# Value products of two attention heads side by side: one PSUM accumulation a pair, softmax denominators on VectorE

## Chip, cores, metric

One core of one Trainium2 chip runs the whole program. The metric is device time in microseconds (us), the median of the runs. The kernel before takes 1075.93 us (three runs, 1074.74 to 1076.09).

## What is computed

Eight batches of eight heads, 512 local and 32 global tokens, head size 64. Every global token attends to all 544 keys; a local token attends to the 32 global keys and to local keys at most 32 positions away. The attention output (4352 rows of 512) then goes through a two-layer network with a softplus between.

```python
s_g = scale * np.matmul(q_g, k_all.transpose(0, 1, 3, 2))
out_g = np.matmul(sm(s_g), v_all)
mask = np.abs(pos[:, None] - pos[None, :]) <= window        # window = 32
s_ll = np.where(mask, scale * (q_l @ k_l^T), -1e9)
a_l = sm(np.concatenate([s_lg, s_ll], axis=-1))
out_l = np.matmul(a_l, np.concatenate([v_g, v_l], axis=2))
...
h = x @ w_in
g = np.maximum(h, 0.0) + np.log1p(np.exp(-np.abs(h)))
return g @ w_out
```

`sm` is a softmax that subtracts the row's maximum and divides by the sum of the exponentials plus 1e-9.

## The kernel before

**Network.** TensorE does the two layers in three products each of single-pass fp32r (L533 to L535 and L556 to L558): high and low halves of each operand, the low by low product left out. Per batch there are 16 steps `f`: `hpart` (12 matmuls of 512 columns into `h`), `act` (L537: Abs, Exp, Ln on ScalarE, one VectorE instruction that reads `h` again, a rounded copy `gh` on ScalarE, and the remainder `gl` on GpSimd), and `opart` (12 matmuls of 512 columns into `o`), two steps behind. In the first batch of the network the weights are still being turned from float64 bit patterns into fp32 halves (L474 to L498, four VectorE instructions a chunk).

**Attention.** Heads are taken two at a time; pair m is heads 2m and 2m+1 of the list of 64, four pairs a batch. Pairs 0 to 3 have code of their own ahead of everything, which the change leaves alone. Pairs 4 to 31 are interleaved with the network. Each is cut into three query windows p = 0, 1, 2 (288, 288 and 192 columns, 32 of them the global queries), and each window has two key chunks of 128 keys. All scores are transposed: keys on partitions, queries on columns.

- `scores(m, p)` (L286): the heads lie on the two row halves (partitions 0 to 63 and 64 to 127) of the operands, four matmuls a window in plain fp32. The result `s_ps` is one PSUM tile of two banks. From pair 8 on VectorE adds the mask while it copies to `s` in SBUF (L315), and a transposing reduction takes the maxima of blocks of 32 keys into `mt` (L316).
- `maxima(m)` (L326): once all three windows are there, GpSimd moves the block maxima to 32 partitions (L329) and VectorE combines them per query (L332 to L339). `probs(m, p)` (L343): a transposing copy spreads them over the partitions (`mb`, L347), GpSimd subtracts (L352 to L355), ScalarE takes the exponential in place (L356).
- `values(m, p)` (L358): two key chunks for each of two heads, four matmuls a window. The stationary operand is the value chunk with a column of ones, 128 by 65, so that row 64 of the result `v_ps` is the denominator. The two heads go to different banks. ScalarE copies the first window to `x` and the rest of the others (L369, L373), and VectorE adds the 64 overlapping queries and the 32 global ones (L374, L375).
- `combine(m)`, `invert(m)`, `normalise(m)`: the denominators go by DMA to `rec_scratch` in DRAM and back as 38 by 32 (`sc`), are inverted (L391, L392), written back, and read once more, broadcast to 64 partitions (`rb`, L396). VectorE multiplies, one instruction a head (L404), into `xa`. The global queries' columns go to `xg_scratch`.

`s_ps` and `v_ps` share one two-bank buffer, tag `a` of `ps_a`, with one copy: each user waits for the previous one to be read.

**Order.** Pieces of attention are written into the stream of network items by due times: `scores(m, p)` at 12m+4p, with maxima and probs behind the third window; `values(m, p)` at 12m+4p+22 (`LAG`); invert 3 and normalise 6 (`STEP`) behind the last. A batch of the network spans 48 units, and `first` (L632) sets the unit at which the second batch starts, so that the four pairs of a batch are normalised by the time `split_x` (L439) makes that batch's operands `xh` and `xl`. Pieces due before 69 (`START`) go ahead of the network. Within an engine the program runs in order; a scheduler places the instructions by its own estimates.

Of the kernel before, what the change touches and what calls it, by code (L numbers as in the profile page):

```python
# [53 lines left out]
def moe_over_global_local_attention(  # L54
# [225 lines left out]
    def load_v(m):  # L280
        t = pl.tile([P, 2, 6, 66], F32, tag="v", name=f"v{m}", bufs=2)
        nc.gpsimd.memset(t[:, :, :, D:D + 1], 1.0)
        nc.sync.dma_start(out=t[:, :, :, 0:D], in_=v[m - M0].rearrange("p (h c d) -> p h c d", h=2, d=D))
        st["v", m] = t

    def scores(m, p):  # L286
# [17 lines left out]
        if p == 0:  # L304
            st["mt", m] = pl.tile([P, 348], F32, tag="mt", name=f"mt{m}", bufs=2)
            nc.gpsimd.memset(windows(st["mt", m], 0, 36, 3, 3), LOW)
# [19 lines left out]
    def maxima(m):  # L326
        mt = st.pop(("mt", m))
# [3 lines left out]
        for u, du, off in ((0, 1, -2), (3, 1, 3)):  # L331
            nc.vector.tensor_reduce(grid(mt, e0 + u, (7, 6), (du, 2)), grid(mt, 3 + u, (12, 6), (du, 2), (off, 2), (GW, 4)), axis=AX.XY, op=ALU.max)  # L332
# [25 lines left out]
    def values(m, p):  # L358
        s, vt = st.pop(("s", m, p)), st["v", m]
        ps = ps_a.tile([P, 2, 512], F32, tag="a", name=f"v_ps{m}_{p}")  # L360
        parts = ((0, 0, 192), (192, 96, 192 if p < 2 else 96))
        for h in range(2):
            for i, (o, qs, w) in enumerate(parts):
                mm(ps[:65, h, qs:qs + w], lhsT=vt[:, h, 2 * p + i, 0:65], rhs=s[:, h, o:o + w],
                   start=i == 0, stop=i == 1, skip_group_check=True)

        if p == 0:
            st["x", m] = pl.tile([65, 2, 608], F32, tag="x", name=f"x{m}", bufs=2)
            nc.scalar.copy(st["x", m][:, :, 0:288], ps[0:65, :, 0:288])  # L369
# [3 lines left out]
        nc.scalar.copy(x[:, :, o + 64:o + w], ps[0:65, :, 64:w])  # L373
        nc.vector.tensor_tensor(x[:, :, o:o + 64], x[:, :, o:o + 64], ps[0:65, :, 0:64], op=ALU.add)  # L374
# [4 lines left out]
    SEG = ((lambda t: t[:, 32:160].unsqueeze(1), 0, 1, 128), (lambda t: windows(t, 192, 224, 2, 192), 128, 2, 192))

    def combine(m):
        nc.sync.dma_start(out=rec_dram[2 * m:2 * m + 2], in_=st["x", m][64:65])

        rows = rec_dram[2 * m:2 * m + 2].rearrange("h (s k) -> (h s) k", k=32)
        sc = pl.tile([38, 32], F32, tag="sc", name=f"sc{m}", bufs=1)
        nc.sync.dma_start(out=sc, in_=rows)
        st["sc", m] = sc, rows

    def invert(m):
        sc, rows = st.pop(("sc", m))  # L390
        after(nc.vector.tensor_scalar(sc, sc, 1e-9, None, op0=ALU.add), "scores")  # L391
        nc.vector.reciprocal(sc, sc)  # L392
        nc.sync.dma_start(out=rows, in_=sc)
# [352 lines left out]
```

## Time and profile before

| | |
|---|---|
| median of the runs | 1075.93 us |
| profiled execution, first to last instruction (span) | 1072.0 us |
| TensorE busy | 1014.0 us, 95% |
| VectorE busy | 596.9 us, 56% |
| ScalarE busy | 546.3 us, 51% |
| GpSimd busy | 460.8 us, 43% |
| mean granted TensorE clock | 0.982 |

The page gives only the span of the profiled execution, no total of its own. The median is 3.9 us above it; that difference is what lies around the span, and it is taken to stay. In the profile PE is TensorE, PEld its weight loads, DVE VectorE, ACT ScalarE, POOL GpSimd, SP the queue of DMA issues. Each plain fp32 matmul shows as two instructions (672 of `v_ps` in the trace for 336 in the program), each fp32r matmul as one. The length of a matmul row includes the way through the array; how much of TensorE's time one takes is read from the distance between starts.

### The profile page before, as it was taken

To read this page: it belongs to the slowest core of one execution; us is meant where nothing else is said; L and a number is where in the kernel's file an instruction comes from. 1 tells how busy PE (TensorE), PEld (TensorE's weight loads), DVE (VectorE), ACT (ScalarE), POOL (GpSimd) and SP (SyncE) were. 2 spreads that over 40 slices of the span, in tenths; PEclk is the share of its full clock that TensorE was granted. 3 is DMA by queue.
4 is the path that set the end of the run, shared out by engine and by line. 5 is a ranking of instruction groups with operands and counts; after the bars stand their busy time and mean duration, and the time that the engine had idled before them with its cause. 6 is when DMAs were issued, how large, how long until landed. Compare 5 with 4: busy or idle time off the path is not lost.

```text
span 1072.0 us, 14176 instructions
## 1 busy us (share of the span) xinstructions
PE 1014.0 (95%) x5108; PEld 801.9 (75%) x5108; DVE 596.9 (56%) x1138; ACT 546.3 (51%) x968; POOL 460.8 (43%) x526
## 2 busy tenths in 40 slices
PE   6895788899999999999999999999999999999996
PEld 4674566677777777777777777777777778888895
DVE  5978698976555655565555654565556542311211
ACT  6856555455445544545444544454444544554452
POOL 2226476653345444445444334544445541322321
PEclk9998899999999999999999999999999999999999
DMA  9523233313221312222221321231222210200000
GB/s 361 169 78 100 97 128 98 96 47 97 51 53 51 95 43 57 49 76 77 57 58 47 97 55 48 55 90 44 57 54 70 67 29 13 72 1 1 10 32 20
DMA packets 78565, 75.05 MB, mean 70 GB/s; under 512 B 53380, under 2 KB 57476, under 8 KB 78496
## 3 DMA queue, kind: packets, MB, share of 16 engines
q1 hardware_dynamic: 77952, 74.09, 23.5%
q8 instruction: 40, 0.66, 0.3%
q14 instruction: 29, 0.24, 0.1%
q10 hardware_dynamic: 544, 0.07, 0.0%
HBM read 64.43 MB, written 9.71 MB: 69 GB/s over the span
## 4 chain that ended last, share of the span: by engine, by line
PE 72%; DVE 10%; DMA 4%; issue 3%; POOL 1%; ACT 1%; SPq 0%; DVEq 0%; POOLq 0%; ACTq 0%
PE h L126 30%; PE o L126 29%; PE v_ps L126 8%; PE s_ps L126 5%; DMA rb<-rec_scratch 3%; DVE xa L404 2%; DVE xl L452 1%; DVE s L315 1%; DMA rec_scratch<-sc 1%; DVE wbitswo L489 1%; DVE xh L451 1%; DVE woraw L492 1%; DVE mb L347 0%; DVE e L543 0%; DVE wbitswo L486 0%
## 5 line engine op out<-in xcount | busy, mean ns | idle before, releaser
L126 PE MATMUL h<-xh,wi 128*128 128x512 f32 (+1 forms) x1152 | 356.4, 393 | 15.7 <-DVE xl L228 9.2
L126 PE MATMUL o<-wo,gh 128*128 128x512 f32 x1088 | 345.1, 398 | 0.0
L547 POOL TENSOR_TENSOR gl<-e,gh 128x512 fp32r<-128x512 f32 x136 | 177.3, 1304 | 386.4 <-ACT gh L546 318.2
L126 PEld LDWEIGHTS h<-xh,wi 128*128 128x128 f32 x1152 | 209.0, 190 | 62.8 <-issue 14.7
L126 PEld LDWEIGHTS o<-wo,gh 128*128 128x128 f32 x1088 | 199.9, 188 | 44.8 <-issue 5.2
L126 PE MATMUL h<-xl,wi 128*128 128x512 f32 (+1 forms) x576 | 220.3, 382 | 2.8 <-DVE xl L452 2.8
L126 PE MATMUL o<-wo,gl 128*128 128x512 f32 x544 | 213.4, 392 | 0.0
L540 ACT ACTIVATE e<-h 128x512 f32<-128x512 f32 x136 | 81.3, 598 | 240.1 <-PE h L126 238.6
L543 DVE SCALAR_TENSOR_TENSOR e<-h,e 128x512 f32<-128x512 f32 x136 | 93.2, 685 | 172.7 <-ACT e L542 167.7
L352 POOL TENSOR_TENSOR s<-s,mb 128x384 f32<-128x384 f32 x112 | 139.0, 1272 | 14.0 <-DVE mb L347 14.0
L546 ACT CAST gh<-e 128x512 fp32r<-128x512 f32 x136 | 83.9, 617 | 97.6 <-DVE e L543 97.5
L126 PEld LDWEIGHTS h<-xl,wi 128*128 128x128 f32 x576 | 109.4, 190 | 27.3 <-DVE xl L452 5.4
L126 PEld LDWEIGHTS o<-wo,gl 128*128 128x128 f32 x544 | 102.2, 188 | 22.8
L126 PE MATMUL v_ps<-s,v 128*65 128x192 f32 (+1 forms) x672 | 114.2, 313 | 4.2 <-DVE s L315 3.9
L126 PEld LDWEIGHTS v_ps<-s,v 128*65 128x65 f32 x672 | 88.5, 137 | 28.0 <-DVE s L315 5.9
L315 DVE TENSOR_TENSOR s<-s_ps,mask 128x768 f32<-128x768 f32 (+1 forms) x96 | 65.0, 696 | 76.6 <-PE s_ps L126 76.6
L356 ACT ACTIVATE s<-s 128x768 f32<-128x768 f32 (+1 forms) x84 | 66.5, 792 | 68.9 <-POOL s L352 45.6
L542 ACT ACTIVATE e<-e,one 128x512 f32<-128x512 f32 x136 | 98.3, 723 | 3.1
L126 PE MATMUL s_ps<-raw 64*128 64x192 f32 (+1 forms) x672 | 78.6, 347 | 14.0 <-issue 9.0
L541 ACT ACTIVATE e<-e 128x512 f32<-128x512 f32 x136 | 85.7, 630 | 3.6
L126 PEld LDWEIGHTS s_ps<-raw 64*128 64x128 f32 x672 | 53.3, 188 | 44.9 <-issue 33.4
L316 DVE TRANSPOSE_TENSOR_REDUCE mt<-s 128x24 f32<-128x768 f32 (+1 forms) x84 | 76.1, 907 | 10.7 <-ACT s L311 8.7
(144 smaller groups left out, 831.7 us busy)
## 6 DMA issues: line engine op xcount, KB each, us to landing
raw<-in_qk SPq DMA_DIRECT2D x56, 272.0 KB
v<-in_v SPq DMA_DIRECT2D x28, 384.0 KB
out<-ot SPq DMA_DIRECT2D x34, 256.0 KB
rb<-rec_scratch SPq DMA_DIRECT2D x28, 304.0 KB
wiraw<-in_w_in SPq DMA_DIRECT2D x16, 512.0 KB
woraw<-in_w_out SPq DMA_DIRECT2D x16, 512.0 KB
raw<-in_qk SPq DMA_DIRECT2D x28, 224.0 KB
v<-in_v SPq DMA_DIRECT2D x4, 512.0 KB
```

Source lines behind the costliest of these rows:

```text
L126: order["pe"] = after(nc.tensor.matmul(*a, **k), "pe").ins
L315: nc.vector.tensor_tensor(s[:, :, o:o + w], ps[:, :, o:o + w], mk.unsqueeze(1).to_broadcast([P, 2, w]), op=ALU.add)
L316: order["scores"] = nc.vector.tensor_reduce(windows(mt, 3 + 12 * p, 36, 2, nb), s.rearrange("p h (b k) -> p h b k", k=32), axis=AX.X, op=A ...
L352: nc.gpsimd.tensor_tensor(sw, sw, windows(mb[:, h], 0, 96, 2, 192), op=ALU.subtract)
L356: nc.scalar.activation(s, s, AF.Exp, scale=0.125)
L404: after(nc.vector.tensor_tensor(y[64 * h:64 * h + 64], x[0:64, h], rb[:, h], op=ALU.mult), "scores")
L540: nc.scalar.activation(e, ph, AF.Abs)
L541: nc.scalar.activation(e, e, AF.Exp, scale=-1.0)
L542: nc.scalar.activation(e, e, AF.Ln, bias=one)
L543: nc.vector.scalar_tensor_tensor(e, ph, 0.0, e, op0=ALU.max, op1=ALU.add)
L546: nc.scalar.copy(gh, e)
L547: nc.gpsimd.tensor_tensor(gl, e, gh.bitcast(F32), op=ALU.subtract)
```

## The change

The value products of a pair become one piece. For each of seven parts (a key chunk with the query columns it serves) there is one matmul a head, with 64 stationary columns and no column of ones. Head 0 writes PSUM partitions 0 to 63, head 1 partitions 64 to 127, at the same columns of the same bank, so that the two use the two column halves of the array. The 608 result columns of a pair lie side by side in two banks (384 and 224): overlapping queries of neighbouring windows add up in PSUM, and only the three copies of the global queries stay apart. The ScalarE copies and the VectorE additions go.

The denominators come from the exponentials in SBUF. `sums(m)` runs a transposing VectorE reduction for each window (the maxima's instruction with add for max), gathers and combines as `maxima` does, adds 1e-9, takes four reciprocals of 32 by 21, and spreads them with one transposing copy to `rb`, 128 by 608, no longer through DRAM. VectorE then multiplies straight out of PSUM, one instruction a bank, into `xa`; GpSimd adds the three copies of the global columns. `rec_scratch`, its four DMAs a pair, and the memset of the ones are gone.

Due times: `sums(m)` at 12m+14, `values(m)` with the multiplication at 12m+21. `first` falls from 72 to 60, so the first batch of the network holds the pieces due from 69 to 108 instead of 69 to 120.

```diff
-LAG = 22
+LAG_Z = 6
+LAG_V = 13
...
     def load_v(m):
-        t = pl.tile([P, 2, 6, 66], F32, tag="v", name=f"v{m}", bufs=2)
-        nc.gpsimd.memset(t[:, :, :, D:D + 1], 1.0)
-        nc.sync.dma_start(out=t[:, :, :, 0:D], in_=v[m - M0].rearrange("p (h c d) -> p h c d", h=2, d=D))
+        t = pl.tile([P, 2, 6, D], F32, tag="v", name=f"v{m}", bufs=2)
+        nc.sync.dma_start(out=t, in_=v[m - M0].rearrange("p (h c d) -> p h c d", h=2, d=D))
...
-    def maxima(m):
-        mt = st.pop(("mt", m))
+    def gather(mt, op):
         for a in range(1, 4):
             nc.gpsimd.tensor_copy(mt[0:32, GW * a:GW * a + GW], mt[32 * a:32 * a + 32, 0:GW])
...
+        return mt[:, e0:e0 + 44]
+
+    def maxima(m):
+        e = gather(st.pop(("mt", m)), ALU.max)
...
-    def values(m, p):
-        s, vt = st.pop(("s", m, p)), st["v", m]
-        ps = ps_a.tile([P, 2, 512], F32, tag="a", name=f"v_ps{m}_{p}")
-        parts = ((0, 0, 192), (192, 96, 192 if p < 2 else 96))
-        for h in range(2):
-            for i, (o, qs, w) in enumerate(parts):
-                mm(ps[:65, h, qs:qs + w], lhsT=vt[:, h, 2 * p + i, 0:65], rhs=s[:, h, o:o + w],
-                   start=i == 0, stop=i == 1, skip_group_check=True)
...
+    def sums(m):
+        zt = pl.tile([P, 348], F32, tag="mt", name=f"zt{m}", bufs=3)
+        nc.gpsimd.memset(windows(zt, 0, 36, 3, 3), 0.0)
+        for p in range(NPC):
+            nb = 12 if p < 2 else 9
+            nc.vector.tensor_reduce(windows(zt, 3 + 12 * p, 36, 2, nb), st["s", m, p].rearrange("p h (b k) -> p h b k", k=32),
+                                    axis=AX.X, op=ALU.add, apply_transpose=True)
+        z = gather(zt, ALU.add)
+        nc.vector.tensor_scalar(z[0:32, 0:42], z[0:32, 0:42], 1e-9, None, op0=ALU.add)
+        zr = pl.tile([P, 21], F32, tag="zr", name=f"zr{m}", bufs=2)
+        for a in range(4):
+            h = a // 2
+            nc.vector.reciprocal(zr[32 * a:32 * a + 32], z[0:32, 21 * h:21 * h + 21])
+        rb = st["rb", m] = pl.tile([P, 608], F32, tag="rb", name=f"rb{m}", bufs=1)
+        nc.vector.transpose(rb.rearrange("p (s k) -> p s k", k=32), zr[:, 1:20].unsqueeze(2).to_broadcast([P, 19, 32]))
+
+    def values(m):
...
+        ps = ps_a.tile([P, 2, 512], F32, tag="a", name=f"v_ps{m}")
+        parts = ((0, 0, 32, 160, 0, 0), (1, 0, 192, 192, 0, 64), (2, 1, 0, 192, 0, 192), (3, 1, 192, 96, 0, 288),
+                 (3, 1, 288, 96, 1, 0), (4, 2, 0, 192, 1, 32), (5, 2, 192, 96, 1, 128))
+        seen = set()
+        for c, p, o, w, bank, at in parts:
+            for h in range(2):
+                mm(ps[64 * h:64 * h + 64, bank, at:at + w], lhsT=vt[:, h, c], rhs=st["s", m, p][:, h, o:o + w],
+                   start=(bank, h) not in seen, stop=(c, bank) in ((3, 0), (5, 1)), skip_group_check=True)
+                seen.add((bank, h))
...
+        for bank, at, w in ((0, 0, 384), (1, 384, 224)):
+            nc.vector.tensor_tensor(y[:, at:at + w], ps[:, bank, 0:w], rb[:, at:at + w], op=ALU.mult)
+        for o in (352, 576):
+            nc.gpsimd.tensor_tensor(y[:, 128:160], y[:, 128:160], y[:, o:o + SG], op=ALU.add)
+        nc.sync.dma_start(out=xg_dram[j, :, SG * b:SG * b + SG], in_=y[:, 128:160])
...
+            ps.append((12 * m + 8 + LAG_Z, lambda m=m: sums(m)))
+            fs = [lambda m=m: values(m)]
...
-    first = end(H // 2 - 1) + 2 * STEP
+    first = end(H // 2 - 1) + STEP
```

**What moves on TensorE.** The order of TensorE before, in the third batch: the first of pair 15's three value pieces (`v_ps15_0`; the number behind a name is a buffer's), which stands twelve network matmuls behind the third score window of pair 16.

```order
L126 MATMUL o2_2_3207<-wo9_1331,gl2_9_3608 128x512
L126 MATMUL o2_3_3211<-wo9_1331,gh2_9_3607 128x512 x2
L126 MATMUL o2_3_3211<-wo9_1331,gl2_9_3608 128x512
L126 MATMUL v_ps15_0_3757<-s15_0_3331,v15_3433 65x192 [waits DMAHW4_49,DVE_49,PE_49]
L126 MATMUL v_ps15_0_3757<-s15_0_3331,v15_3433 65x192 x3
L126 MATMUL h2_12_3764<-xh2_0_3053,wi12_1365 128x512 x2
L126 MATMUL h2_12_3764<-xl2_0_3054,wi12_1365 128x512
```

The same place in the order after: the last score matmuls of pair 16, then six network matmuls, then all of pair 15's value products.

```order
L125 MATMUL s_ps16_2_3918<-raw16_2_3688 128x96 x2
L125 MATMUL h2_15_3911<-xh2_2_3045,wi15_1626 128x512 x2
L125 MATMUL h2_15_3911<-xl2_2_3046,wi15_1626 128x512
L125 MATMUL h2_15_3911<-xh2_3_3051,wi15_1626 128x512 x2
L125 MATMUL h2_15_3911<-xl2_3_3052,wi15_1626 128x512
L125 MATMUL v_ps15_3970<-s15_0_3556,v15_3513 64x160 [waits DMAHW6_49,DVE_49,PE_49]
L125 MATMUL v_ps15_3970<-s15_0_3556,v15_3513 64x160
L125 MATMUL v_ps15_3970<-s15_0_3556,v15_3513 64x192 x2
L125 MATMUL v_ps15_3970<-s15_1_3633,v15_3513 64x192 x2
L125 MATMUL v_ps15_3970<-s15_1_3633,v15_3513 64x96 x4
L125 MATMUL v_ps15_3970<-s15_2_3684,v15_3513 64x192 x2
L125 MATMUL v_ps15_3970<-s15_2_3684,v15_3513 64x96 x2
```

Three pieces have become one, the two heads alternate, and the cover between the scores and the value products that reuse their buffer is six matmuls instead of twelve.

**What moves on VectorE.** The order of VectorE before, between the reading of the first and of the second score window of pair 16 (`s16_0`, `s16_1`; `e2_8` is the softplus of network step 8).

```order
L315 TENSOR_TENSOR s16_0_3564<-s_ps16_0_3557,mask_72 128x768 [waits PE_49]
L316 TENSOR_REDUCE mt16_3562<-s16_0_3564 128x2x12 [waits DVE_49]
L543 SCALAR_TENSOR_TENSOR e2_8_3544<-h2_8_3531,e2_8_3544 128x512 [waits Activation_49]
L374 TENSOR_TENSOR x14_3529<-x14_3529,v_ps14_1_3588 65x2x64 [waits DMAHW4_49,Activation_49]
L375 TENSOR_TENSOR x14_3529<-x14_3529,v_ps14_1_3588 65x2x32
L543 SCALAR_TENSOR_TENSOR e2_9_3602<-h2_9_3581,e2_9_3602 128x512 [waits Activation_49]
L315 TENSOR_TENSOR s16_1_3628<-s_ps16_1_3623,mask_72 128x768 [waits PE_49]
```

After, the end of the same stretch one pair earlier (pairs 14 and 15): `zt14` and `zr14` are the denominators of pair 14.

```order
L367 TENSOR_REDUCE zt14_3580<-s14_1_3394 128x2x12 [waits Activation_49]
L367 TENSOR_REDUCE zt14_3580<-s14_2_3445 128x2x9 [waits Activation_49]
L329 TENSOR_REDUCE zt14_3580<-zt14_3580 32x6x2 [waits DVE_49,Pool_49]
L329 TENSOR_REDUCE zt14_3580<-zt14_3580 32x6x2
L330 TENSOR_REDUCE zt14_3580<-zt14_3580 32x6x2
L332 TENSOR_REDUCE zt14_3580<-zt14_3580 32x2
L333 COPY zt14_3580<-zt14_3580 32x6 [waits DVE_49]
L533 SCALAR_TENSOR_TENSOR e2_9_3607<-h2_9_3573,e2_9_3607 128x512 [waits Activation_49]
L370 TENSOR_SCALAR zt14_3580<-zt14_3580 32x42 [waits DVE_49]
L374 RECIPROCAL zr14_3594<-zt14_3580 32x21 [waits DVE_49]
L374 RECIPROCAL zr14_3594<-zt14_3580 32x21 x3
L313 TENSOR_TENSOR s15_1_3633<-s_ps15_1_3628,mask_72 128x768 [waits PE_49]
```

The denominators stand ahead of the reading of pair 15's second score window and of a softplus, and they wait for ScalarE (the exponentials) and for GpSimd (the gather) there.

**What moves ahead of the network.** VectorE's last operand for the network's first matmul is the second `xl0_3`. Before:

```order
L489 SCALAR_TENSOR_TENSOR wbitswi6_798<-wiraw6_160,wbitswi6_798 128x512 [waits DMAHW3_49,DVE_49]
L486 TENSOR_SCALAR wbitswi9_1057<-wbitswi9_1057 128x512 [waits Activation_49]
L347 STREAM_TRANSPOSE mb5_0_839<-mt5_763 128x576 [waits DVE_49,Pool_49]
L488 TENSOR_SCALAR wbitswi8_1011<-wbitswi8_1011 128x512 [waits DVE_49]
L492 SCALAR_TENSOR_TENSOR wiraw6_160<-wiraw6_160,wbitswi6_798 128x512 [waits DVE_49]
L228 TENSOR_TENSOR xl0_3_780<-o0_3_1_858,xh0_3_779 64x256 x2
```

After, the rows that end in the same instruction:

```order
L367 TENSOR_REDUCE zt4_768<-s4_2_721 128x2x9 [waits Activation_49]
L476 TENSOR_SCALAR wbitswi9_1105<-wbitswi9_1105 128x512 [waits DMAHW3_49,PE_49]
L479 SCALAR_TENSOR_TENSOR wbitswi6_817<-wiraw6_158,wbitswi6_817 128x512 [waits DMAHW3_49,DVE_49]
L347 STREAM_TRANSPOSE mb5_0_858<-mt5_761 128x576 [waits DVE_49]
L478 TENSOR_SCALAR wbitswi8_1046<-wbitswi8_1046 128x512 [waits DVE_49]
L478 TENSOR_SCALAR wbitswi9_1105<-wbitswi9_1105 128x512 [waits DVE_49]
L482 SCALAR_TENSOR_TENSOR wiraw6_158<-wiraw6_158,wbitswi6_817 128x512 [waits DVE_49]
L227 TENSOR_TENSOR xl0_3_799<-o0_3_1_877,xh0_3_798 64x256 x2
```

The three denominator reductions of pair 4 (the last of them is the first row here) and one more weight instruction now stand ahead of it.

More of the change, by code (lines that the diff above doesn't have):

```diff
@@ L27 @@
 EW = (0, 544, 1088)
-XOFF = (0, 224, 448)
 NF = DFF // P
@@ L377, in moe_over_global_local_attention @@
-    xa, ready = {}, set()
[L379 to L393, printed above, removed]
-        rb = pl.tile([64, 2, 608], F32, tag="rb", name=f"rb{m}", bufs=1)
-        r = rec_dram[2 * m:2 * m + 2]
-        nc.sync.dma_start(out=rb, in_=r.unsqueeze(0).to_broadcast([64, 2, 608]))
-        st["rb", m] = rb
@@ L399, in normalise @@
-    def normalise(m):
-        b, j = divmod(m, H // 2)
-        x, rb = st.pop(("x", m)), st.pop(("rb", m))
-        y = xa[b, j] = pl.tile([P, 608], F32, tag="xa", name=f"xa{b}_{j}", bufs=4)
-        for h in range(2):
-            after(nc.vector.tensor_tensor(y[64 * h:64 * h + 64], x[0:64, h], rb[:, h], op=ALU.mult), "scores")
-        nc.sync.dma_start(out=xg_dram[j, :, SG * b:SG * b + SG], in_=y[:, 160:192])
+    xa, ready = {}, set()
+    SEG = ((lambda t: t[:, 0:128].unsqueeze(1), 0, 1, 128), (lambda t: windows(t, 160, 224, 2, 192), 128, 2, 192))
@@ new lines, in values @@
+    def values(m):
+        b, j = divmod(m, H // 2)
+        vt = st.pop(("v", m))
+        ps = ps_a.tile([P, 2, 512], F32, tag="a", name=f"v_ps{m}")
[7 more added lines that the diff above has]
+                seen.add((bank, h))
+        for p in range(NPC):
+            del st["s", m, p]
+        rb = st.pop(("rb", m))
+        y = xa[b, j] = pl.tile([P, 608], F32, tag="xa", name=f"xa{b}_{j}", bufs=4)
+        for bank, at, w in ((0, 0, 384), (1, 384, 224)):
[3 more added lines that the diff above has]
+        nc.sync.dma_start(out=xg_dram[j, :, SG * b:SG * b + SG], in_=y[:, 128:160])
@@ L426, in pieces @@
                 ps.append((12 * m + 4 * p, piece(*fs)))
[L427 to L434 removed]
+            ps.append((12 * m + 8 + LAG_Z, lambda m=m: sums(m)))
+            fs = [lambda m=m: values(m)]
+            if m + 2 < M:
+                fs.append(lambda m=m: load_v(m + 2))
+            ps.append((end(m), piece(*fs)))
         ps.sort(key=lambda t: t[0])
@@ L739 @@
     args.append(nc.dram_tensor("xg_scratch", (4, P, B * SG), F32, kind="Internal").ap())
-    args.append(nc.dram_tensor("rec_scratch", (B * H, 608), F32, kind="Internal").ap())
     args.append(nc.dram_tensor("out_0", (B * S, DM), F32, kind="ExternalOutput").ap())
```

29 lines of the change are left out of this document (5 added, 24 removed).

## The prediction

> **What bounds the kernel now.** I read the page's first part, then busy time by stage, then TensorE's timeline over one pair.
>
> ```profile
> PE 1014.0 (95%) x5108; PEld 801.9 (75%) x5108; DVE 596.9 (56%) x1138; ACT 546.3 (51%) x968; POOL 460.8 (43%) x526
> ```
> ```profile
> 150.00:200.00 50.00, 40.63 (x204) 30.84 (x203) 43.97 (x70) 29.73 (x51) 33.41 (x28) 0.97 0.32 97
> ```
> ```profile
> 250.00:870.00 620.00, 616.19 (x3086) 483.96 (x3085) 348.57 (x687) 304.08 (x502) 284.66 (x338) 1.00 0.23 62
> ```
>
> The columns after the length are busy us of PE, PEld, DVE, ACT, POOL. From 250 to 870 us TensorE is busy 616.2 of 620 us: there, time taken from TensorE comes off the end, and ScalarE (49%) and GpSimd (46%) have room. In the first batch (150 to 200 us) VectorE at 44.0 of 50 us is the fuller engine: TensorE time freed there is not simply won.
>
> What a value piece costs is read from starts, in TensorE's timeline.
>
> ```profile
> 515.26 0.39 PE L126 MATMUL h<-xl,wi 128*128 128x512 f32 x1
> 515.49 1.14 PE L126 MATMUL v_ps<-s,v 128*65 128x192 f32 x8
> 516.41 0.71 PE L126 MATMUL o<-wo,gh 128*128 128x512 f32 x2
> 516.96 0.39 PE L126 MATMUL o<-wo,gl 128*128 128x512 f32 x1
> ...
> 520.41 0.40 PE L126 MATMUL h<-xl,wi 128*128 128x512 f32 x1
> 520.74 0.79 PE L126 MATMUL s_ps<-raw 64*128 64x192 f32 x8
> 521.46 0.73 PE L126 MATMUL h<-xh,wi 128*128 128x512 f32 x2
> 522.03 0.39 PE L126 MATMUL h<-xl,wi 128*128 128x512 f32 x1
> ...
> 524.80 0.39 PE L126 MATMUL o<-wo,gl 128*128 128x512 f32 x1
> 525.04 0.62 PE L126 MATMUL o<-wo,gh 128*128 128x512 f32 x2
> 525.49 0.40 PE L126 MATMUL o<-wo,gl 128*128 128x512 f32 x1
> 525.73 1.46 PE L126 MATMUL v_ps<-s,v 128*65 128x192 f32 x8
> 526.89 0.76 PE L126 MATMUL h<-xh,wi 128*128 128x512 f32 x2
> 527.49 0.39 PE L126 MATMUL h<-xl,wi 128*128 128x512 f32 x1
> ```
>
> Network matmuls start 0.23 us apart (524.80 to 525.49 is three). From 525.49 to 527.49 lie three of them and a value piece of the first window: 2.00 - 0.69 = 1.31 us. The third window: 516.96 - 515.26 - 0.69 = 1.01 us. The second has the first's widths, so a pair's value products take 2 x 1.31 + 1.01 = 3.63 us. A third score window takes 522.03 - 520.41 - 0.69 = 0.93 us.
>
> **The change on TensorE.** The next rows are the timeline's answers for two narrow windows in a value piece and one in a score piece.
>
> ```profile
> 525.73 0.33 PE L126 MATMUL v_ps<-s,v 128*65 128x192 f32 x1
> ```
> ```profile
> 525.73 0.49 PE L126 MATMUL v_ps<-s,v 128*65 128x192 f32 x2
> ```
> ```profile
> 520.74 0.43 PE L126 MATMUL s_ps<-raw 64*128 64x192 f32 x2
> ```
> ```profile
> 521.01 0.52 PE L126 MATMUL s_ps<-raw 64*128 64x192 f32 x6
> ```
>
> A second value instruction ends 0.16 us after the first: 192 columns take 0.16 us, 0.83 ns a column, and a plain fp32 matmul is two such passes. In the score piece two instructions start at 520.74 together: the heads sit on the two row halves of the array and run at once. Its streams are 2 x 0.16 + 2 x 0.08 = 0.48 us for both heads against 0.93 us taken, so 0.45 us go into changing to half-array work and back. One part of that shows: the second couple starts 0.27 us after the first, not 0.16, its weights not yet there.
>
> After, each head has 160 + 192 + 192 + 96 + 96 + 192 + 96 = 1024 columns (1056 before), 2 x 1024 x 0.83 ns = 1.71 us a head. No row shows column halves. The bounds: both heads at once, 1.71 us, or one after the other, 3.41 us. I take the first, because the row halves, the nearest row, do run at once in the same data type with the same alternation of heads. The way in and out lies between 0 (the 65-column piece costs 1.31 us for eight times 0.16) and 0.45 us; I take 0.45, the half-array row. So 1.71 + 0.45 = 2.16 us a pair, 1.47 us less.
>
> The Trainium skill, "TensorEngine Tiling (Array Packing)", Tiling Modes, says that changing the mode drains TensorE: the 0.45 us agree. The Trainium skill, "TensorE: Matmul & The Clock Gate", Measured speedup vs the span model, gives 2.38 times for three column tiles, 79% of the ideal, which no run here shows; an estimate from that figure would be 3.41 / 1.59 + 0.45 = 2.60 us a pair, and the time 1054 us.
>
> By the orders, 71 value windows lie behind the first batch before (24 pairs less one first window) and 24 pairs after: 24 x 3.63 - 1.31 = 85.8 us become 24 x 2.16 = 51.8 us. Three score windows move out of the first batch into this stretch (it now ends at unit 108, not 120), at about 1.0 us each. Net: 34.0 - 3.0 = 31.0 us less.
>
> **On VectorE and the others.** Rows by shape:
>
> ```profile
> L543 DVE SCALAR_TENSOR_TENSOR e<-h,e 128x512 f32<-128x512 f32 x136 | 93.2, 685 | 172.7 <-ACT e L542 167.7 <-POOL gl L547 5.0
> ...
> L404 DVE TENSOR_TENSOR xa<-x,rb 64x608 f32<-64x608 f32 x56 | 69.0, 1232 | 22.3 <-DMA rb<-rec_scratch 21.9
> L316 DVE TRANSPOSE_TENSOR_REDUCE mt<-s 128x24 f32<-128x768 f32 x56 | 54.5, 972 | 3.2 <-ACT s L311 2.0
> ...
> L315 DVE TENSOR_TENSOR s<-s_ps,mask 128x768 f32<-128x768 f32 x48 | 45.2, 942 | 26.5 <-PE s_ps L126 26.5
> ...
> L347 DVE STREAM_TRANSPOSE mb<-mt 128x576 f32<-128x576 f32 x56 | 40.4, 757 | 0.9
> ...
> L316 DVE TRANSPOSE_TENSOR_REDUCE mt<-s 128x18 f32<-128x576 f32 x28 | 21.7, 777 | 7.5 <-ACT s L311 6.7
> ...
> L329 POOL COPY mt<-mt 32x75 f32<-32x75 f32 x84 | 21.4, 254 | 58.3 <-DVE sc L391 54.3 <-DVE mt L316 1.6
> ...
> L374 DVE TENSOR_TENSOR x<-x,v_ps 65x128 f32<-65x128 f32 x56 | 15.8, 283 | 118.4 <-ACT x L373 118.4
> L332 DVE TENSOR_REDUCE mt<-mt 32x12 f32<-32x96 f32 x56 | 15.2, 308 | 14.9 <-POOL mt L329 14.8
> ...
> L315 DVE TENSOR_TENSOR s<-s_ps,mask 128x384 f32<-128x384 f32 x24 | 13.3, 555 | 50.1 <-PE s_ps L126 50.1
> ...
> L392 DVE RECIPROCAL sc<-sc 38x32 f32<-38x32 f32 x28 | 9.6, 344 | 0.8
> ```
> ```profile
> 549.49 0.43 PE L126 MATMUL s_ps<-raw 64*128 64x192 f32 x2
> ```
>
> Added a pair: reductions 2 x 0.97 + 0.78 = 2.72; five small gather steps and the addition at up to 0.31 = 1.8; four reciprocals at up to 0.34 = 1.4; the spreading copy, 608 columns by the 576 row, 0.80; two multiplications of 384 and 224 columns out of PSUM, 0.56 and about 0.4. Together 7.7 us. Removed: 2 x 1.23 + 2 x 0.28 + two smaller additions below 0.28 + reciprocal and addition (0.34 and less), about 4.1. VectorE gains some 3.6 us a pair. A pair's period is 549.49 - 520.74 = 28.75 us (third score window to third score window); busy for 56% of it, VectorE has 12.6 us free. That cover holds the cost at nothing as long as nobody waits for VectorE in turn. ScalarE loses three copies. GpSimd gets a second gather (three copies of 0.25 us) and two additions of 32 columns, each about such a copy: 1.3 us a pair, at 46%. The DMAs that go (four a pair) were waited for by VectorE only at `rb`, 21.9 us in 27 waits, beside other work.
>
> A new wait: `v_ps` has six matmuls, 1.38 us, behind `s_ps` instead of twelve, and takes the same buffer, so VectorE's reading must fit beneath.
>
> ```profile
> 521.58 0.82 DVE L315 TENSOR_TENSOR s<-s_ps,mask 128x384 f32<-128x384 f32 x2 [2.95 <-PE s_ps L126]
> ```
>
> It ends at 522.40, 1.66 us after `s_ps` starts at 520.74; the value piece comes at 0.93 + 1.38 = 2.31 us. That leaves 0.65 us. I put 1 us in all on places where VectorE is late.
>
> **The first batch.** Two rows bound it: TensorE's longest wait, and a step of the chain of waits.
>
> ```profile
> PE h L126 <- DVE xl L228: 9.2, 1, 9.2
> ```
> ```profile
> 235.46 3.87 DMA rb<-rec_scratch
> ```
>
> The network's first matmul waits for `xl`, and pair 4's reductions (2.72 us) and a weight instruction now stand ahead of that: about 3 us later. Against it, TensorE loses three score windows and 13 x 1.2 - 4 x 2.16 = 7.0 us of value products there, and the wait for `rb`, 3.87 us on the chain at the batch's end, goes. If TensorE were the limit the batch would be 10 us shorter; if the weights on VectorE are, with the 3 us and denominators, up to 6 us longer. I take 2 us shorter, near the VectorE end because of the 44 of 50 us.
>
> **The sum**, against the profiled span: 1072.0 - 31.0 - 2.0 + 1.0 = 1040.0 us, and with the 3.9 us around it 1043.9 us.
>
> **Rivals.**
>
> *The heads take turns.* If the column halves do not run at once, a pair costs 3.41 + 0.45 = 3.86 us, 24 pairs 92.6 us against 85.8: 6.8 more, 3.0 for the scores, less 2.0, plus 1.0: 1084.7 us, slower. Its place is the 28 value pieces, its price 1.7 us a pair, and it decides from the point where less than a fifth of one head's stream overlaps the other's (a pair at 3.49 us or more gives no gain in the sum). For it: no row shows two column halves, and each needs its own moving columns on all 128 rows, where the row halves share the 128. Against it: fp32r streams 512 columns in 0.23 us, twice as fast as fp32, so the operand path can carry two fp32 streams. Chance 0.11.
>
> *Weights are loaded in the open.* If each couple must wait for its weights as the second score couple does, 0.27 - 0.16 = 0.11 us at 13 further steps are 1.43 us: 3.59 us a pair, 24 pairs 86.2 us, time 1078.3 us, about the bound of no change. Against it:
>
> ```profile
> 525.49 0.70 PEld L126 LDWEIGHTS v_ps<-s,v 128*65 128x65 f32 x4
> ```
>
> The first of these loads starts at 525.49, with the matmul before it, although both use all 128 rows. The Trainium skill, "TensorE: Matmul & The Clock Gate", The mechanism, says that loads overlap running matmuls only where the row group differs, which here it does not between the heads; by that rule this rival would hold, and for the full array the trace disagrees. Chance 0.07.
>
> *VectorE comes late.* After scores the denominators wait for the exponentials, the gather, then stand ahead of the next reading.
>
> ```profile
> 534.60 0.68 ACT L356 ACTIVATE s<-s 128x576 f32<-128x576 f32 x1 [0.68 <-POOL mt L306]
> ```
>
> The last exponential ends at 535.28, 14.5 us behind `s_ps`. Reduction 0.8, GpSimd 0.8 to 2 (three copies, behind another piece of work at worst), gather and reciprocals 3.2, a softplus 0.7, the next window's reading and maxima 1.9, spreading 0.8, another softplus 0.7 end near 24 us; the pair's period is 28.75 - 1.47 = 27.3 us. Some 3 us are left. Each us beyond them costs every pair one: at 1 us beyond, 24 us, 1068 us. Chance 0.10, still faster as a rule.
>
> **How the numbers follow.** Forecast 0.72, at 1031 us (no cost of the way in and out, 24 x 0.45 = 10.8, and a little of the first batch) to 1057 us (first batch 6 us longer, 5 us of waits for VectorE). The range goes on to 1070 us for the VectorE rival and leaves out the other two, 0.18. A measurement of this kernel can tell about 0.2%, 2.2 us. Faster: the forecast and most of the VectorE rival, 0.81. Same: most of the open weights, 0.06. Slower: taking turns, and a little of the others, 0.13.
>
> **What would show it.** Right: `v_ps` rows of 64 columns in couples that start together, and a piece of about 2.2 us; PE still over 98% from 250 to 870 us; VectorE near 70% there; no rows of `rec_scratch`. Wrong: starts 0.16 us apart throughout (taking turns), 0.27 us (weights), or idle PE ahead of `v_ps` and `s_ps` put down to DVE L313 (VectorE). A first batch that ends later by more than 6 us would be an error in that term alone.

## The result, and the profile after

The changed kernel takes 1036.45 us (median of 4 runs, 1034.49 to 1037.52) beside 1076.01 us of the kernel before in the same session (1074.74 to 1077.86). The ratio is 0.9628, with a 95% interval of 0.9613 to 0.9644. The profiled spans are 1032.6 and 1072.0 us, 39.4 us apart; the forecast was 32.

The first part of the page after, and two rows of its busy time by stage (after the length: busy us of PE, PEld, DVE, ACT, POOL):

```profile
PE 973.4 (94%) x5220; PEld 763.2 (74%) x5220; DVE 691.6 (67%) x1362; ACT 507.4 (49%) x884; POOL 471.6 (46%) x666
```
```profile
150.00:200.00 50.00, 42.38 (x210) 32.16 (x209) 47.60 (x76) 29.55 (x50) 33.64 (x38) 0.90 0.23 73
...
250.00:870.00 620.00, 611.79 (x3301) 476.83 (x3300) 440.67 (x894) 287.62 (x458) 304.17 (x470) 1.00 0.17 50
```

TensorE has 41 us less work and still fills 98.7% of the long stretch; VectorE rises from 56% to 71% there. In the first batch VectorE is fuller still, 47.6 of 50 us.

TensorE's timeline over one pair's value products, and the answers for two narrow windows at their start:

```profile
521.33 0.40 PE L125 MATMUL h<-xl,wi 128*128 128x512 f32 x1
521.66 1.96 PE L125 MATMUL v_ps<-s,v 128*64 128x160 f32 x28
523.55 0.74 PE L125 MATMUL o<-wo,gh 128*128 128x512 f32 x2
524.13 0.40 PE L125 MATMUL o<-wo,gl 128*128 128x512 f32 x1
```
```profile
521.66 0.36 PE L125 MATMUL v_ps<-s,v 128*64 128x160 f32 x2
```
```profile
521.66 0.49 PE L125 MATMUL v_ps<-s,v 128*64 128x160 f32 x4
```

From 521.33 to 524.13 lie three network starts (0.69 us) and the piece: 2.80 - 0.69 = 2.11 us, forecast 2.16. Two instructions start within the first 0.04 us, and in the trace all 28 start in couples, the second of a couple 6 to 7 ns behind the first: both heads run at once. The second couple has started when the window ends, 0.24 us after the first. The piece's 28 weight loads, in the weight engine's timeline, lie inside the piece:

```profile
521.66 1.77 PEld L125 LDWEIGHTS v_ps<-s,v 128*64 128x64 f32 x28 [0.37 <-issue]
```

Where the 39.4 us came from shows in the starts of ScalarE's first operation on `h`. It occurs 136 times, 16 a batch, so the 17th is the first step of batch 1. ScalarE's timeline before, and after:

```profile
245.83 0.60 ACT L540 ACTIVATE e<-h 128x512 f32<-128x512 f32 x1 [0.96 <-PE h L126]
```
```profile
231.85 0.58 ACT L530 ACTIVATE e<-h 128x512 f32<-128x512 f32 x1
```

The first batch gave 14.0 us. The 113th such row (first step of batch 7) starts at 932.1 and 891.4 us, so from batch 1 to there it gave 686.3 - 659.5 = 26.8 us; the rest, 139.9 before and 141.2 after, gave 1.3 us back. Forecast were 2 us for the first batch and 30 for the stretch behind it.

The waits of TensorE that are left (us in total, times, longest):

```profile
PE h L125 <- DVE xl L227: 11.5, 1, 11.5
PE v_ps L125 <- ACT s L309: 10.4, 2, 6.4
PE v_ps L125 <- issue: 8.2, 5, 1.9
PE h L125 <- DVE e L533: 5.5, 4, 3.0
```

The two long waits ahead of `v_ps` are in the first batch (from 136 and from 176 us on); pairs whose scores ScalarE reads (L309) stand ahead of them. The five short ones are one in each of five batches behind it; this is one in TensorE's timeline, and the same place in VectorE's:

```profile
326.66 0.40 PE L125 MATMUL h<-xl,wi 128*128 128x512 f32 x1
328.63 1.96 PE L125 MATMUL v_ps<-s,v 128*64 128x160 f32 x28 [1.58 <-issue]
```
```profile
324.54 1.51 DVE L441 CAST xh<-xa 128x128 fp32r<-128x128 f32 x2 [1.15 <-PE h L125]
325.97 1.83 DVE L442 TENSOR_TENSOR xl<-xa,xh 128x128 fp32r<-128x128 f32 x2
327.72 0.81 DVE L313 TENSOR_TENSOR s<-s_ps,mask 128x384 f32<-128x384 f32 x2
```

The score matmuls of this pair started at 324.67. Their reading (L313) comes only at 327.72 because the next batch's operands are split first (L441, L442). `v_ps` takes the buffer that is read there, so it starts 0.1 us after the reading ends at 328.53. "issue" means that the profile names no releaser; the order of times does.

### The profile page after: what moved, and what is told of

Read it like the earlier page. It is cut to its first block, busy times and chain, and to the rows that moved or that the text cites. A ratio compares the mean times of both kernels' runs of the same rounds, so it can differ in the third digit from the quotient of the medians.

```text
span 1032.6 us, 14525 instructions
## 1 busy us (share of the span) xinstructions
PE 973.4 (94%) x5220; PEld 763.2 (74%) x5220; DVE 691.6 (67%) x1362; ACT 507.4 (49%) x884; POOL 471.6 (46%) x666
## 4 chain that ended last, share of the span: by engine, by line
PE 76%; issue 1%; DVE 0%; ACT 0%; POOL 0%
PE o L125 33%; PE h L125 33%; PE s_ps L125 5%; PE v_ps L125 4%; DVE e L533 0%; ACT ot L555 0%; DVE zt L329 0%; POOL zt L326 0%; DVE zt L330 0%; DVE zt L332 0%
## 5 line engine op out<-in xcount | busy, mean ns | idle before, releaser
L125 PE MATMUL h<-xh,wi 128*128 128x512 f32 (+1 forms) x1152 | 350.5, 388 | 18.0 <-DVE xl L227 11.5
L537 POOL TENSOR_TENSOR gl<-e,gh 128x512 fp32r<-128x512 f32 x136 | 180.3, 1326 | 317.9 <-ACT gh L536 258.0
L533 DVE SCALAR_TENSOR_TENSOR e<-h,e 128x512 f32<-128x512 f32 x136 | 92.6, 681 | 164.7 <-ACT e L532 159.5
L352 POOL TENSOR_TENSOR s<-s,mb 128x384 f32<-128x384 f32 x112 | 112.5, 1036 | 38.3 <-DVE mb L347 38.3
L313 DVE TENSOR_TENSOR s<-s_ps,mask 128x768 f32<-128x768 f32 (+1 forms) x96 | 64.7, 694 | 26.0 <-PE s_ps L125 25.3
L347 DVE STREAM_TRANSPOSE mb<-mt 128x576 f32<-128x576 f32 (+1 forms) x84 | 56.3, 696 | 35.3 <-POOL s L352 34.5
L125 PE MATMUL v_ps<-s,v 128*64 128x96 f32 (+2 forms) x784 | 58.4, 303 | 18.6 <-ACT s L309 10.4
```

What stands on the lines that cost most here:

```text
L125: order["pe"] = after(nc.tensor.matmul(*a, **k), "pe").ins
L313: nc.vector.tensor_tensor(s[:, :, o:o + w], ps[:, :, o:o + w], mk.unsqueeze(1).to_broadcast([P, 2, w]), op=ALU.add)
L347: nc.vector.transpose(mb[:, :, :QW[p]].rearrange("p h (s k) -> p h s k", k=32), windows(e, 7 * p, 21, 2, k).unsqueeze(3).to_broadcast([P, ...
L352: nc.gpsimd.tensor_tensor(sw, sw, windows(mb[:, h], 0, 96, 2, 192), op=ALU.subtract)
L533: nc.vector.scalar_tensor_tensor(e, ph, 0.0, e, op0=ALU.max, op1=ALU.add)
L537: nc.gpsimd.tensor_tensor(gl, e, gh.bitcast(F32), op=ALU.subtract)
```

## The experiments

Theory, as the runs set out to test it: most of the gain is the two column halves running at once, and the rest came from the first batch, where VectorE's load, not TensorE's, sets the length. Rivals: due times alone do it; the dropped round trip does it; TensorE's shorter work does it in the first batch too. All kernels ran beside the kernel before (1076.0 to 1076.8 us). The table shows the starts of the 17th and 113th row, as above, and spans and medians in us; the experiments are named E1 to E7 (edits of the changed kernel) and B1 to B3 (edits of the kernel before).

Starts and spans come from one profiled execution each, and that lies between 2.0 us below its kernel's median (changed kernel) and 2.7 above (E2). How far two such executions part by themselves shows ahead of the network's first softplus. Up to there the changed kernel and E2 run the same instructions in the same order on all four engines, as do E3 and E5; yet this softplus starts at 101.6 and 104.4 us, and at 99.7 and 101.5 us. Before and B1 differ there by one instruction on GpSimd and start it at 98.3 and 96.5 us. So 2 to 3 us of a difference in the 17th row can be chance.

| kernel | 17th | 113th | span | median | ratio to before (95%) |
|---|---|---|---|---|---|
| before | 245.8 | 932.1 | 1072.0 | 1076.01 | |
| changed | 231.9 | 891.4 | 1032.6 | 1036.45 | 0.9613 to 0.9644 |
| E1 heads in turn | 232.9 | 923.2 | 1064.1 | 1065.95 | 0.9872 to 0.9925 |
| E2 `first` at 72 | 248.9 | 904.8 | 1046.1 | 1045.12 | 0.9677 to 0.9731 |
| E3 values due at 14 | 229.4 | 880.0 | 1021.0 | 1023.47 | 0.9485 to 0.9530 |
| E4 no denominators | 228.5 | 886.6 | 1027.6 | 1029.43 | 0.9538 to 0.9588 |
| E5 due at 14, `first` at 72 | 236.9 | 891.4 | 1032.4 | 1033.13 | 0.9584 to 0.9619 |
| E6 values due at 15 | 239.4 | 899.8 | 1040.9 | 1042.59 | 0.9674 to 0.9703 |
| E7 due at 14, no denominators | 227.5 | 879.1 | 1020.1 | 1022.41 | 0.9484 to 0.9513 |
| B1 no round trip | 240.1 | 918.5 | 1058.4 | 1060.56 | 0.9840 to 0.9885 |
| B2 values due at 14 | 245.6 | 931.5 | 1071.4 | 1073.27 | 0.9959 to 0.9986 |
| B3 due at 14, no round trip | 248.1 | 941.8 | 1081.7 | 1083.98 | 1.0062 to 1.0095 |

**E1, the heads in turn.** All matmuls of one column half are issued ahead of the other's.

```diff
-        for c, p, o, w, bank, at in parts:
-            for h in range(2):
+        for h in range(2):
+            for c, p, o, w, bank, at in parts:
```

> The changed kernel with one loop turned round: all seven parts of head 0, then all seven of head 1, so that neighbouring matmuls lie on the same column half. Theory (the gain is that both column halves run at once): a value piece goes from 2.1 us to 2 x 1.71 + 0.4 = 3.8 us, 28 times 1.7 us are 48 us, some of it hidden in the first batch: 1075 to 1085 us, about the kernel before. Rival (the gain comes from the shorter way of the denominators, the dropped copies and the new due times): within 5 us of the changed kernel's 1036 us.

1065.95 us, between the two ranges: 29.5 us of the 40 go. TensorE's timeline over a piece:

```profile
506.80 0.40 PE L125 MATMUL h<-xl,wi 128*128 128x512 f32 x1
507.12 3.27 PE L125 MATMUL v_ps<-s,v 128*64 128x160 f32 x28
510.32 0.73 PE L125 MATMUL o<-wo,gh 128*128 128x512 f32 x2
510.89 0.40 PE L125 MATMUL o<-wo,gl 128*128 128x512 f32 x1
```

510.89 - 506.80 - 0.69 = 3.40 us, 1.29 more than in the changed kernel; 24 times this is 31 us. The cause holds. The expected time was too high for two reasons. At the change of head the halves still overlap: in the trace the second head's first matmul starts at 508.432 us and the first head's last at 508.835. And the first batch ends only 1.0 us later though four pieces there cost 5.2 us more. TensorE's waits of over 0.15 us in that batch fall from 16.5 to 10.0 us: most of the added time went into them.

**E2, the first batch as long as before.** `first`, which sets the end of the first batch 48 units later, goes back from 60 to 72, so a pair's pieces return to the first batch.

```diff
-    first = end(H // 2 - 1) + STEP
+    first = end(H // 2 - 1) + STEP + 12
```

> The changed kernel with 12 added to first, so that the first batch of the network again holds the pieces due up to unit 120: three more score windows and one more value piece. Theory (the first batch ends when TensorE's work is done, so a piece costs the same there and later): 1036 us, give or take 3. Rival (the first batch is VectorE's, as the prediction had it): the moved pieces bring VectorE some 9 to 15 us there and the time rises by 5 us or more.

1045.12 us: the expectation of no change fell. Batch 1 begins 17 us later in the profiles, and the stretch to batch 7 gives back 3.6 us. The largest wait, in TensorE's timeline and then in VectorE's:

```profile
226.95 0.40 PE L125 MATMUL o<-wo,gl 128*128 128x512 f32 x1
234.53 3.68 PE L125 MATMUL v_ps<-s,v 128*64 128x160 f32 x28 [7.18 <-issue]
```
```profile
228.44 1.16 DVE L374 RECIPROCAL zr<-zt 32x21 f32<-32x21 f32 x4
229.63 1.57 DVE L441 CAST xh<-xa 128x128 fp32r<-128x128 f32 x2
231.12 0.80 DVE L376 STREAM_TRANSPOSE rb<-zr 128x608 f32<-128x608 f32 x1
231.85 1.24 DVE L442 TENSOR_TENSOR xl<-xa,xh 128x128 fp32r<-128x128 f32 x2
...
233.62 0.81 DVE L313 TENSOR_TENSOR s<-s_ps,mask 128x384 f32<-128x384 f32 x2
```

The reading of the scores (L313) stands behind denominators (L374, L376) and the split (L441, L442), and `v_ps` begins when it ends. So the 17 us mix the work put back with waits for VectorE. They hold some chance too: by the medians E2 is 8.7 us above the changed kernel, which with the 3.6 us given back leaves about 12 for the first batch. The edit also thins the cover there: by the trace six network matmuls stand between the third score window and the value products in three of four places, where the changed kernel has twelve.

**E3, the value products due one unit later.** Twelve instead of six network matmuls then stand between the third score window and the value products.

```diff
-LAG_V = 13
+LAG_V = 14
```

> The changed kernel with LAG_V at 14 for 13, which puts twelve network matmuls instead of six between the third score window and the value piece. Theory (once a batch the operand split on VectorE delays the reading of the scores, and the value piece waits 1.7 us for the buffer): five such waits go, 8 us less, 1028 us. Rival (the wait has another cause, or moves to the next score window, which now comes 18 instead of 24 matmuls behind): 1036 us, give or take 2.

1023.47 us, faster than both kernels and 4.5 us below the theory's figure. The long stretch in the windows of E3, and VectorE's timeline where a batch's operands are split:

```profile
250.00:870.00 620.00, 620.00 (x3353) 483.59 (x3352) 441.91 (x907) 296.89 (x469) 306.33 (x474) 1.00 0.17 50
```
```profile
321.31 0.82 DVE L313 TENSOR_TENSOR s<-s_ps,mask 128x384 f32<-128x384 f32 x2 [0.65 <-PE s_ps L125]
322.17 0.78 DVE L314 TRANSPOSE_TENSOR_REDUCE mt<-s 128x18 f32<-128x576 f32 x1
322.87 1.44 DVE L441 CAST xh<-xa 128x128 fp32r<-128x128 f32 x2
```

TensorE has no gap left: 620 of 620 us. The later due time did two things: more cover, and the reading now stands ahead of the split (L441) in VectorE's queue. From batch 1 to batch 7 it gives 659.5 - 650.6 = 8.9 us, about the five waits (8.2). The first batch gave 2.5 us more; no run says why, and it is within what two executions can differ by.

**E4, no denominators.** The value products are multiplied by a constant instead.

```diff
-        zt = pl.tile([P, 348], F32, tag="mt", name=f"zt{m}", bufs=3)
...
-        nc.vector.transpose(rb.rearrange("p (s k) -> p s k", k=32), zr[:, 1:20].unsqueeze(2).to_broadcast([P, 19, 32]))
+        st["rb", m] = ones
```

> The changed kernel without its denominators: sums is left out and the multiplication takes a constant, so the softmax is not normalised in pairs 4 to 31. VectorE loses about 7 us a pair, some 190 us in all. Theory (that work lies beside TensorE): only the waits at the batch boundaries (8 us) and the later start of the network (3 us) can go: 1025 to 1034 us. Rival (VectorE is the second limit): below 1015 us.

1029.43 us: denominators on VectorE cost 7.0 us by the medians, 5.0 by the spans, and 3.4 of these in the first batch. That is within the theory's range, but not by its path, for the five waits behind the first batch stay, as the waits of E4 show:

```profile
PE v_ps L125 <- issue: 8.1, 5, 1.6
```

So they do not come from the denominators; in the rows above it is the split of the operands that stands ahead of the reading. From the network's first softplus to batch 1 VectorE is busy 14.1 us less than in the changed kernel (104.5 and 118.6 us by the windows of the two traces), and this stretch is 2.0 us shorter (128.3 and 130.3 us). So VectorE's busy time alone does not set its length: that part of the theory fell.

**B1, before without the round trip.** The reciprocals by way of DRAM are left out in the same manner.

```diff
-        nc.sync.dma_start(out=rec_dram[2 * m:2 * m + 2], in_=st["x", m][64:65])
...
-        nc.sync.dma_start(out=rb, in_=r.unsqueeze(0).to_broadcast([64, 2, 608]))
-        st["rb", m] = rb
+        st["rb", m] = st["ones"]
```

> The kernel before without its way through DRAM: combine and invert are left out and the multiplication takes a constant, so the softmax is not normalised in pairs 4 to 31; the value products stay as they were. Theory (the DMA round trip holds up the operand split at the batch boundaries): five waits of 1.2 us and some 4 to 6 us at the end of the first batch go: 1062 to 1068 us. Rival (the round trip is hidden): 1076 us, give or take 2.

1060.56 us, 1.4 below the theory's range: the round trip cost 16 us by the medians, 13.6 by the profiled spans: 5.7 up to batch 1 (1.8 of them ahead of the network's first softplus, where the two kernels differ by one GpSimd instruction alone), and 7.9 from batch 1 to batch 7. Before, TensorE waited twice in each of five of those batches, 0.40 us for `xl` and 0.37 us for the scores' reading. Both waits are gone, and a batch takes 114.6 us from start to start where it took 116.0. The 1.2 us of the expectation is not what the waits show.

**B2, before with its values due at 14 instead of 22.**

```diff
-LAG = 22
+LAG = 14
```

> The kernel before with LAG at 14 for 22: value pieces eight units earlier, first at 64 for 72, so the first batch holds pieces up to unit 112. Theory (TensorE's work is the same, wherever it stands): 1073 to 1079 us. Rival (the shorter first batch of the changed kernel comes from the due times): 1068 us or less.

1073.27 us: due times alone are not the gain. Nor is a first batch shorter just because it holds less: this one holds two score windows and two value pieces fewer, and batch 1 begins at 245.6 us beside 245.8.

**E5, due at 14 with the long first batch.** E2's edit without its thin cover: `first` is 72, as in E2 (61 in E3). By the traces twelve network matmuls, once 18, stand between the third score window and the value products in the first batch; the changed kernel has twelve there, E3 18.

```diff
-LAG_V = 13
+LAG_V = 14
...
-    first = end(H // 2 - 1) + STEP
+    first = end(H // 2 - 1) + STEP + 11
```

> The changed kernel with the value products at due time 14 (twelve network matmuls instead of six between the third score window and the value products, as in the run that gave 1023.5 us), and the first batch as long, to within one unit, as in the run that put it back to unit 72 (1045.1 us; batch 1 began there at 248.9 us, against 231.9 in the changed kernel and 229.4 with due time 14 alone). Two theories of why the first batch of the changed kernel is 14 us shorter and not 2. Theory of the work moved: the pieces that the shorter first batch leaves to later cost VectorE time there, whatever the place of the value products; then batch 1 begins at 243 to 248 us, and the whole takes 1030 to 1036 us. Theory of the wait: most of the 17 us of the earlier run was the value products standing behind a late VectorE in TensorE's queue, with six matmuls of cover; then batch 1 begins at 233 to 240 us and the whole takes 1022 to 1028 us.

Batch 1 begins at 236.9 us, 7.5 later than in E3 and 5.0 later than in the changed kernel, as the theory of the wait has it: of E2's 17 us (about 12 by the medians), 5 to 7.5 are the pair put back, and the rest was waiting or chance. The whole, 1033.13 us, missed that theory's range. The edit shifts the pieces behind the first batch too: there 18 network matmuls stand ahead of the value products and 12 behind them, where E3 has 12 and 18. A new wait stands in each of five batches, ahead of the next scores; TensorE's timeline and VectorE's:

```profile
340.69 0.40 PE L125 MATMUL o<-wo,gl 128*128 128x512 f32 x1
342.33 0.92 PE L125 MATMUL s_ps<-raw 64*128 64x192 f32 x8 [1.25 <-issue]
```
```profile
340.06 1.44 DVE L347 STREAM_TRANSPOSE mb<-mt 128x576 f32<-128x576 f32 x2
341.42 0.82 DVE L395 TENSOR_TENSOR xa<-v_ps,rb 128x384 f32<-128x384 f32 x2
```

The scores need the buffer that L395 reads; L395 stands behind the spreading of the maxima (L347) and ends at 342.24.

**E6, due at 15.** 24 matmuls of cover ahead of the value products, 12 behind them.

```diff
-LAG_V = 13
+LAG_V = 15
```

> The changed kernel with the value products at due time 15: 24 network matmuls between the third score window and the value products, 12 from there to the next scores, which take the same buffers. Due time 13 gave 1036.45 us with five waits of 1.7 us ahead of the value products behind the first batch, due time 14 gave 1023.5 us with none. If those waits were all that the due time touches, 15 gives nothing more: 1021 to 1026 us, and no wait ahead of v_ps. Rival: the wait moves to the next scores, which must wait until VectorE has read the value products out of the same buffer under 12 matmuls (2.8 us): idle TensorE ahead of s_ps, 1026 to 1036 us.

1042.59 us: the rival, and more of it than its range. The wait moved to the scores. Three such waits stand in the first batch, 20.9 us in all; by the trace only six matmuls lie behind the value products there. This is the longest, in TensorE's timeline, and what VectorE did in it:

```profile
150.01 1.01 PE L125 MATMUL s_ps<-raw 64*128 64x192 f32 x4 [10.24 <-issue]
```
```profile
138.36 2.21 DVE L476 TENSOR_SCALAR wbitswo<-wbitswo 128x512 f32<-128x512 f32 x3
...
141.85 3.04 DVE L478 TENSOR_SCALAR wbitswo<-wbitswo 128x512 int32<-128x512 int32 x3
144.81 2.68 DVE L479 SCALAR_TENSOR_TENSOR wbitswo<-woraw,wbitswo 128x512 int32<-128x512 int32 x3
...
148.48 0.54 DVE L395 TENSOR_TENSOR xa<-v_ps,rb 128x384 f32<-128x384 f32 x1
```

The reading of the value products (L395) stands behind three rows of weight steps (three instructions and 2.2 to 3.0 us each), and TensorE waits 10.2 us for it. Against E3 the first batch lost 10.0 us and the stretch to batch 7 another 9.8, where 0.2 us ahead of the scores and 1.15 us for the softplus (L533) come back batch after batch.

**E7, due at 14 and no denominators.** E4's edit, and with it:

```diff
-LAG_V = 13
+LAG_V = 14
```

> The changed kernel with the value products at due time 14 and without the denominators: the reductions, the gather, the reciprocals and the spreading copy are left out, and the value products are multiplied by a constant, so that the softmax isn't normalised. At due time 13 leaving them out gave 7.0 us. If the denominators cost VectorE time in the first batch, it is again 5 to 8 us: 1015 to 1019 us. If they cost only by making VectorE late ahead of the value products, the doubled cover has taken most of that: 1020 to 1024 us.

1022.41 us. Against E3 that is 1.1 us less, and the two intervals overlap: with more cover the denominators' 7 us are down to what this comparison can hardly tell. That fits a cost by lateness, not by busy time, as the second theory has it; which wait it is the runs don't show, for the two traces' waits in the first batch come to 15.1 us in E3 and 16.1 us in E7.

**B3, B1 and B2 together.** B1's edit, and with it:

```diff
-LAG = 22
+LAG = 14
```

> The kernel before with the value products due at 14 and without the round trip of the denominators through DRAM (the reciprocals and the broadcast are left out and the value products are multiplied by a constant, so that the softmax isn't normalised). Separately these gave 1073.3 and 1060.6 us, against 1076.6. If they add, 1057 us (1055 to 1059). Beside the changed kernel at due time 14 without denominators this leaves the column halves as the only large difference: 24 pairs at 3.63 less 2.1 us in the full stretch is 36 us, less what the first batch hides; I expect 36 to 42 us between the two, with the first batch's share. Rival: about 31 us, as the run with the heads in turn gave.

1083.98 us, 27 above the expected sum and 0.8% slower than the kernel before. The two edits don't add. TensorE's timeline at one of five new waits, and ScalarE's:

```profile
359.46 0.92 PE L126 MATMUL s_ps<-raw 64*128 64x192 f32 x8 [1.90 <-ACT x L369]
```
```profile
358.26 0.62 ACT L537 CAST gh<-e 128x512 fp32r<-128x512 f32 x1 [2.27 <-DVE e L534]
358.78 0.63 ACT L369 COPY x<-v_ps 65x576 f32<-65x576 f32 x1
```

ScalarE's copy that empties `v_ps` stands behind a cast that waits 2.27 us for VectorE. Against B1, batch 1 begins 8.0 us later and the five waits are 9.5 us; where some 6 us more behind the first batch come from stays open. With this miss, B3 against E7 (61.6 us) says nothing of the column halves. E4 against B1 does better, both without denominators and with their own due times: 31.1 us, beside E1's 29.5, though these two differ in the dropped copies and additions as well.

## Why the prediction was right, and where it was not

**What held.** TensorE is the bound from batch 1 on, and the value products of a pair fell to 2.11 us (forecast 2.16: 1.71 of streams, and 0.40 instead of 0.45 for the way in and out). 24 pieces of 2.11 are 50.6 us against 51.8. VectorE's load per pair rose by 3.4 us (forecast 3.6): 348.57 us x 29.01 / 620 = 16.3 before, 440.67 x 27.77 / 620 = 19.7 after, with a pair's period from the starts of batches 2 to 6. Rows of 64 columns start in couples, and no row of `rec_scratch` is left.

**The rivals.** Taking turns is refuted by the rows of two starts and priced by E1: it gave 1066 us, not 1085, still 1% faster than before, since the first batch gave more than the working had, and the halves overlap at the change of head. Open weights are refuted: the 28 loads fit into the piece, and behind the second couple no step is late. The Trainium skill, "TensorE: Matmul & The Clock Gate", The mechanism, lets a load overlap only where the row group differs, in its list of what overlaps (ahead of the list it allows a background weight buffer too); the two heads here use the same rows, and the 28 loads do overlap, within the piece's 1.96 us. The estimate from the same page's three column tiles (Measured speedup vs the span model), 2.60 us a pair, was too high too: two halves gave 1.71 us of streams for 3.41, all of the factor two. VectorE late for every pair is refuted by the waits of the changed kernel: behind the first batch `v_ps` waits in five of 24 pairs, 8.2 us in all, and `s_ps` in none.

**The step that failed** is the first batch, "2 us shorter, near the VectorE end because of the 44 of 50 us". It was 14.0. The working let VectorE eat most of what TensorE saved. From the network's first softplus to batch 1 the two traces show otherwise. TensorE is busy 125.4 us before and 114.7 after, the 10 us less that the working had. But its time not busy, which should have grown, fell as well, from 22.1 to 15.5 us. With the start 3.3 us later, that makes the 14.0. VectorE was busy 122.8 of 147.5 us before, so it was not full, and 118.6 us after: with the denominators in and the moved pieces out it has 4.2 us less to do.

What the working overlooked shows in TensorE's waits before. Five stand ahead of scores in the first batch, 13.9 us in all; after the change none does. The largest row of the waits, then one of them in TensorE's timeline and the same place in the chain of waits (start, length, what):

```profile
PE s_ps L126 <- issue: 9.0, 3, 4.6
```
```profile
198.87 0.79 PE L126 MATMUL s_ps<-raw 64*128 64x192 f32 x8 [2.10 <-issue]
```
```profile
197.75 0.69 DVE wbitswi L489
198.44 0.19 DVE x L374
198.63 0.13 DVE x L375
```

The scores take the buffer that the overlap additions (L374, L375) read, and these stand behind a weight step (L489). All five waits end 0.1 us after such an L375, an instruction that the change drops; B1 keeps it, and four of the waits with it (12.5 us). In their place come 10.4 us ahead of `v_ps` (2.4 before). This is an order of times in the traces. The chain of waits in this stretch before goes through VectorE for 60.7 us, TensorE for 29.1 and the round trip's DMAs for 10.4, so not every wait of TensorE lies on it; and no run leaves out the additions alone. Whether they are the cause, and what they are worth, is not shown.

What the runs do show is what is not the cause alone. 5.2 us of TensorE's time cost 1.0 there (E1), 14.1 us of VectorE's gave 2.0 (E4), a first batch of the kernel before with fewer pieces was no shorter (B2). One pair put back costs 5.0 us against the changed kernel (E5), close to the working's price on TensorE, 3.0 + 2.16 us. The round trip's wait, 3.87 us, the working named but put into neither of its bounds; B1 prices it at 3.9 to 5.7 us there. B3 shows that such parts don't simply add, so they are not summed here.

**Three smaller steps.** The waits for `rb` "beside other work" was wrong: without the round trip the kernel before gained 16 us (B1). "1 us in all on places where VectorE is late" was too small: 8.2 us by the waits, because the margin of 0.65 us came from an ordinary pair and not from the pair that meets the operands' split; E3 recovers 8.9 us there. And the late start, forecast at 3 us because of pair 4's denominators, came (98.3 to 101.6 us for the first softplus), but how much of it is theirs is not shown: without them it starts at 100.2 (E4), with them at 99.7 in E3 and 104.4 in E2.

**Why the sum came near all the same.** The first batch gave 12 us more than forecast, the stretch behind it 3 less (26.8 instead of 30), the end 1.3 less. That the stretch came so near is in part luck: two terms were mis-sized there and nearly cancel, the waits for VectorE (8.2 us instead of 1.0) and the round trip (7.9 us by B1, instead of nothing). The 3.9 us added to the span were too many by about 2: the changed kernel's profiled execution took 1034.49 us with a span of 1032.6.

## What to carry to other kernels

Where TensorE fills a stretch, price a change there by the starts of its instructions. Where no engine fills it, busy times price little: list TensorE's waits there with what ends them, ask which of those instructions the change adds or removes, and test each by removing it alone. A margin taken from an ordinary iteration has to be looked at again where another loop's work meets it: one unit more of due time was worth 13 us here, and one more than that lost 19. Two edits to a schedule in which engines wait for a shared buffer need not add: B1 gave 16 us and B2 3, and both together cost 7. Measure the pair.

## What the runs showed of the hardware

- Two fp32 matmuls on the two column halves, on the same 128 rows with moving columns of their own, run at once at the full rate of each: 1024 columns a head, two passes at 0.83 ns a column, for both heads in 2.11 us with the way in and out.
- They overlap without alternating in the order of issue: with the heads in turn (E1), the second half's first matmul started 0.40 us ahead of the first half's last one (508.43 and 508.84 us).
- The second couple of a piece starts 0.19 us after the first, though the 160 columns of the first take 0.14 (the third couple follows the second by that); after it no couple is late (0.16 us a step of 192 columns, 0.08 of 96), although every matmul loads its own weights.
